# One maximum over two score banks: PSUM as one tile of eight banks in a fused attention and feed-forward kernel

## The chip, the core and the metric

One core of a Trainium2 chip runs the whole program. The metric is the device time of one execution in microseconds (us). Lower is better.

The engines are named as in the profile. PE is TensorE, with PEld for its weight loads. DVE is VectorE, ACT is ScalarE, POOL is GpSimd, and SP issues the DMAs. PSUM is the memory that PE writes its results to: eight banks, of which one holds 512 float32 numbers in each of 128 partitions.

## The reference

Attention over 8 batches of 12 heads, 448 positions, 64 numbers a head, followed by a feed-forward layer over all 3584 positions:

```python
q_n, k_n = rmsnorm(q, g_q), rmsnorm(k, g_k)          # over the last axis
scores = (q_n @ k_n.T) / sqrt(64)
scores = scores - max(scores, axis=-1)
attn = exp(scores); attn = attn / (sum(attn, axis=-1) + 1e-9)
x = (attn @ v)                                       # heads joined: 3584 x 768
h = relu(x @ w_in)                                   # 768 x 2048, float64 weights
out = (s * h * h + b) @ w_out                        # 2048 x 768
```

## The kernel before

The kernel works on 48 pairs of heads, six pairs to a batch. A pair has eight steps (`W = 8`), four for each of its two heads. One Python loop over the step number `s_`, from -16 on, writes out the order of the work of every engine by hand, and each engine then runs its own queue strictly in that order. What is called "step s" below is one turn of this loop.

For each pair the scores are computed twice. The first time is only for the maxima. `score(i)` multiplies a block of 112 queries of one head with all 448 keys of that head (PE L453) into a PSUM bank (`sh`), and `maximum(i)` takes the negated maximum of each query out of it (DVE L464) into one column of `nmx`. A pair has eight such blocks, `i = 8 * pair + 0 ... 7`, and this holds for the first twelve pairs (`TURNED = 12`). `shift` then sends four columns at a time by DMA into a row of `qb`. The second time, `score_t(s)` computes one transposed block of 128 keys by 448 queries, with the maxima already subtracted (PE L496 and L499, bank `st`), `exponent(s)` takes the exponential (ACT L511), and `weigh(s - 2)` multiplies with the values, summing four steps in one bank `av` (PE L557, two instructions a step). `take` copies `av` out (ACT L568, L572, L573).

Queries and keys come in as rows. `norm_rows` scales them (ACT L255, DVE L260, POOL L263, L264 and L269), `turn` transposes them on PE into two banks (`tk`, L282, two groups of four), and `split_turned` makes the high and low parts out of the two banks (ACT L290, L291 and L292; one step later DVE L294 and L295). For four steps at a time this runs at a fixed distance: the transposes in a step that is 2 more than a multiple of 4, L290 to L292 in the next step, L294 and L295 in the step after, which is a multiple of 4.

Beside this, DVE turns pieces of the float64 weights `w_in` into float32 parts (`convert`, DVE L149, L152, L154 and L157 for each piece, 24 pieces), and from step 56 on the feed-forward matmuls of the batch before (PE L198, names `ph`) fill PE's queue between the others. So during the first six pairs, steps 0 to 47 and some more, PE has no such filler.

The order inside one step is: `score_t`, filler, `exponent`, what was begun earlier (L260, L294, L295 among it), the jobs of the step (turns among them), `score`, filler, `maximum`, the late jobs (`convert` among them), `weigh`, filler.

A block's step is `i - AHEAD` with `AHEAD = 10`. The first 20 blocks have steps of their own in `SHIFTED`: 0 to 19 stand at -9, -8, -7, -6, -4, -3, -2, -1, 1, 1, 2, 2, 4, 4, 5, 5, 8, 8, 9, 10.

A bank is taken by `psum()`, which pops the one that stands first in the list `free`, and is appended to the list again where the code gives it back. Because the list is one queue over all uses, a PE instruction into a bank waits for the last reader of whatever used that bank before: an `exponent` (ACT), a `take` (ACT), an L295 (DVE) or a `maximum` (DVE).

Of the kernel before, what the change touches and what calls it, by code (L numbers as in the profile page):

```python
# [9 lines left out]
F32 = mybir.dt.float32  # L10
# [3 lines left out]
ALU = mybir.AluOpType  # L14
AX = mybir.AxisListType
# [10 lines left out]
AHEAD = 10  # L26
# [11 lines left out]
SHIFTED = {0: -9, 1: -8, 2: -7, 3: -6, 4: -4, 5: -3, 6: -2, 7: -1, 8: 1, 9: 1, 10: 2, 11: 2, 12: 4, 13: 4, 14: 5, 15: 5, 16: 8, 17: 8, 18: 9, 19: 10}  # L38
# [13 lines left out]
PLAIN = 11  # L52

THIRD = (11, 14, 17)

PACE_OUT = tuple(48 * b + 16 + 8 * i for b in range(2, 8) for i in range(4))

# [4 lines left out]
def attention_then_relu2_ffn(  # L62
# [30 lines left out]
    V, S, G, T = nc.vector, nc.scalar, nc.gpsimd, nc.tensor  # L93

    NPAIR, P, _, SEQ = kq.shape
# [10 lines left out]
    QC = SEQ // NQ  # L106
# [16 lines left out]
    wpool = ctx.enter_context(tc.tile_pool(name="wpool", bufs=1))  # L123
    dpool = ctx.enter_context(tc.tile_pool(name="dpool", bufs=1, space=DRAM))
    ps = ctx.enter_context(tc.tile_pool(name="ps", bufs=1, space=PSUM))
    free = [f"bank{i}" for i in range(8)]

    ident = cpool.tile([P, P], F32, name="ident")
    make_identity(nc, ident)
# [11 lines left out]
    def psum(name):  # L141

        bank = free.pop(0)
        return ps.tile([P, 512], F32, tag=bank, name=name), bank

    def to_single(w, a, m):

# [29 lines left out]
    def parts_of_w_in():  # L177

        for i in range(NS):
            whi[i] = wpool.tile([P, NCC, FS], F32R, tag=f"wh{i}", name=f"wih{i}")  # L180
            wlo[i] = wpool.tile([P, NCC, FS], F32R, tag=f"wl{i}", name=f"wil{i}")
            for c0 in range(0, FS, WI):
                for cc in range(NCC):
                    f0 = 2 * (i * FS + c0)
                    src = w_in32[cc * P : (cc + 1) * P, f0 : f0 + 2 * WI]
                    yield whi[i][:, cc, c0 : c0 + WI], wlo[i][:, cc, c0 : c0 + WI], src
# [4 lines left out]
    def ffn_in(xs, b, fcs):  # L191

        phs = [psum(f"ph{b}_{fc}") for fc in fcs]
        for cc in range(NCC):
            for (ph, bank), fc in zip(phs, fcs):
                i, f0 = divmod(fc * P, FS)
                for m, (w, part) in enumerate(((whi[i], 0), (wlo[i], 0), (whi[i], 1))):
                    T.matmul(  # L198
                        ph[:, :SEQ],
                        w[:, cc, f0 : f0 + P],  # L200
                        xs[b, cc][:, part, :],
                        start=cc == 0 and m == 0,
                        stop=cc == NCC - 1 and m == 2,
                    )
                    if cc == NCC - 1 and m == 2:
                        later.append((ph, bank, b, fc))
                    yield
# [22 lines left out]
    with tc.tile_pool(name="apool", bufs=1) as ap:  # L230
        khs = {}
        raws, kqs, invs, vrs, nmxs, shs, tks = ({} for _ in range(7))
# [38 lines left out]
        def turn(p, j):  # L271
            raw = raws.pop((p, j))
            if p >= APART:
                tk, bank = tks[p, j] = psum(f"tk{p}_{j}")
                for c in range(NQ):
                    x = raw[:, c].rearrange("p t d -> p (t d)")
                    T.transpose(tk[:, c * QC : (c + 1) * QC], x, ident[:QC, :QC])
                return
            for t in range(2):
                tk, bank = psum(f"tk{p}_{j}_{t}")  # L280
                for c in range(NQ):
                    T.transpose(  # L282
                        tk[:D, c * QC : (c + 1) * QC], raw[:, t, c], ident[:QC, :QC]
                    )
                tks[p, j, t] = tk[:D, :SEQ], bank
# [151 lines left out]
        def score(i):  # L437

            p, c = divmod(i, W)
            j, c = divmod(c, NQ)  # L440
            sh, bank = psum(f"sh{i}")
            a = slice(j * SEQ, (j + 1) * SEQ)
            shs[i] = sh, bank
            if p >= TURNED:
                q, k = qz, khs.get(p)
                if i % W != 3:
                    q = qa[p % 2][:, a][:, :WHOLE].rearrange("k (p c) -> k c p", c=3)[:, c]
                    k = ka[p % 2][:, a]
                else:
                    khs.pop(p)  # L450
                T.matmul(sh[:, :SEQ], q, k, start=True, stop=True)  # L451
                return
            T.matmul(  # L453
                sh[:QC, :SEQ], qa[p % 2][:, a].rearrange("k (p c) -> k c p", c=NQ)[:, c],
                ka[p % 2][:, a], start=True, stop=True,
            )

        def maximum(i):
            p, c = divmod(i, W)
            if c == 0:  # L460
                nmxs[p] = bounds.tile([P, W], F32R, tag="nmx", bufs=2, name=f"nmx{p}")
            sh, bank = shs.pop(i)
            n = QC if p < TURNED else P
            V.tensor_reduce(  # L464
                out=nmxs[p][:n, c : c + 1], in_=sh[:n, :SEQ], op=ALU.max, axis=AX.X, negate=True
            )
            free.append(bank)
# [158 lines left out]
        def pieces():  # L626
            for i, (hi, lo, src) in enumerate(parts_of_w_in()):
                if i in THIRD:
                    w = ap.tile([P, WI, 2], I32, tag="low", name=f"w64i{i}")
# [72 lines left out]
        def at(s_, f, *a):  # L702
            jobs[s_].append((f, a))

        for i, s_ in enumerate(PACE):
            if i != THIRD[-1]:
                at(s_ + 3, load_piece)
# [64 lines left out]
        scores = {}  # L772
        for i in range(NSLOT):
            if i // W >= TURNED and i % W == W - 1:
                continue
            scores.setdefault(SHIFTED.get(i, i - AHEAD), []).append(i)

        def within(i):
            return 0 <= i < NSLOT
# [2 lines left out]
        with tc.manual_schedule(engines=ORDERED):  # L782
            begun = []
            for s_ in range(FIRST, NSLOT + START + NCC):
# [20 lines left out]
                for i in scored:  # L805
                    score(i)
# [4 lines left out]
                for i in scored:  # L811
                    maximum(i)
# [14 lines left out]
    with tc.tile_pool(name="opool", bufs=1) as op:  # L827
# [153 lines left out]
        with tc.manual_schedule(engines=ORDERED):  # L981
# [29 lines left out]
            for n in range(7 * NG):  # L1011
                g, k = divmod(n, 7)
# [78 lines left out]
```

## Time and profile before

| what | value |
|---|---|
| time, median of 3 runs | 1376.97 us (1376.26 to 1377.02) |
| span of the profiled execution, first to last instruction | 1375.6 us |
| median less span (launch and end around the span) | 1.4 us |
| PE busy in the span | 1363.6 us (99%) |
| DVE busy in the span | 1057.3 us (77%) |
| ACT busy in the span | 937.2 us (68%) |
| granted TensorE clock over the span | 1.000 |

The page gives no other time of the profiled execution than its span, so the median is set beside the span here. PE's matmuls are pipelined, so that a busy share of 99% doesn't say that PE never waits: how far the starts of its instructions lie apart says more. The same holds for DVE, where the record of an instruction lasts some 0.08 us longer than it keeps the next one away.

### The profile page before, as it was taken

The page shows a single profiled execution, that of the slowest core. Times are in us where ns is not written, and L with a number is a line of the kernel's source. Part 1 is how long each engine was busy: PE and PEld are TensorE (multiplying, and loading weights), DVE is VectorE, ACT ScalarE, POOL GpSimd, SP SyncE. Part 2 cuts the span into 40 slices and gives each one's busy share as a digit, 9 for nine tenths or more (in the row PEclk, how much of TensorE's full clock was granted, in tenths as well). Part 3 has the DMA queues.
Part 4 walks back from the last instruction along what each step waited for, and adds up shares of the span by engine and source line. Part 5 has one row for each costly group of instructions (what it writes and reads, how often), then busy time and mean ns, then how long its engine had stood idle before and what let it go on. Part 6 is the DMA issues. An engine that isn't in the chain of part 4 may idle for free.

```text
span 1375.6 us, 21578 instructions
## 1 busy us (share of the span) xinstructions
PE 1363.6 (99%) x6970; PEld 1255.6 (91%) x6970; DVE 1057.3 (77%) x1572; ACT 937.2 (68%) x1727; POOL 603.1 (44%) x486
## 2 busy tenths in 40 slices
PE   8999999999999999999999999999999999999998
PEld 7767789999999999999999999999999999999998
DVE  7999997897888798688788878526766676666763
ACT  6886778888888888888888887636544434344431
POOL 6875787766667666676667665100000000000000
PEclk9999999999999999999999999999999999999999
DMA  4555676787788788778778867356543332343330
GB/s 133 150 145 169 181 232 197 230 249 214 223 235 239 222 243 232 221 222 250 229 220 240 236 204 211 104 197 222 186 119 118 88 91 90 95 121 112 85 90 35
DMA packets 262800, 243.39 MB, mean 177 GB/s; under 512 B 85280, under 2 KB 244000, under 8 KB 262688
## 3 DMA queue, kind: packets, MB, share of 16 engines
q1 hardware_dynamic: 262688, 242.03, 60.0%
q8 instruction: 55, 0.90, 0.3%
q14 instruction: 57, 0.47, 0.1%
HBM read 177.21 MB, written 53.38 MB: 168 GB/s over the span
## 4 chain that ended last, share of the span: by engine, by line
PE 92%; DVE 4%; ACT 2%; DMA 1%; issue 1%; SPq 0%; POOL 0%; DVEq 0%; POOLq 0%; ACTq 0%
PE ph L198 32%; PE p L936 30%; PE av L557 15%; PE st L496 5%; PE st L499 5%; PE sh L451 4%; PE sh L453 1%; DVE nmx L464 1%; PE tk L282 1%; DVE wai L154 1%; DVE ssq L260 0%; DVE wai L152 0%; DVE wai L157 0%; DMA zb<-z_d 0%; ACT e L511 0%
## 5 line engine op out<-in xcount | busy, mean ns | idle before, releaser
L198 PE MATMUL ph<-x,wih 128*128 128x448 f32 x1536 | 488.3, 365 | 0.0
L198 PEld LDWEIGHTS ph<-x,wih 128*128 128x128 f32 x1536 | 289.0, 188 | 28.7 <-issue 6.1
L198 PE MATMUL ph<-x,wil 128*128 128x448 f32 x768 | 293.3, 382 | 0.0
L515 ACT ACTIVATE st<-st 128x448 f32<-128x448 f32 (+1 forms) x296 | 155.9, 527 | 104.1 <-PE st L499 102.7
L464 DVE TENSOR_REDUCE nmx<-sh 128x1 fp32r<-128x448 f32 (+1 forms) x348 | 212.8, 616 | 12.0 <-PE sh L451 6.3
L538 DVE TENSOR_TENSOR low<-st,ah 128x448 fp32r<-128x448 f32 x222 | 136.7, 616 | 47.2 <-ACT ah L523 42.5
L557 PE MATMUL av<-ah,vs 128*128 128x448 f32 x592 | 168.7, 366 | 0.0
L496 PE MATMUL st<-qa,ka 128*128 128x448 f32 (+1 forms) x384 | 159.1, 414 | 2.3 <-DVE nmx L464 2.2
L198 PEld LDWEIGHTS ph<-x,wil 128*128 128x128 f32 x768 | 144.3, 188 | 17.0 <-issue 6.2
L523 ACT CAST ah<-st 128x448 fp32r<-128x448 f32 (+1 forms) x296 | 156.9, 530 | 2.0
L499 PE MATMUL st<-qb,kb 128*128 128x448 f32 (+1 forms) x384 | 140.3, 365 | 0.0
L557 PEld LDWEIGHTS av<-ah,vs 128*128 128x128 f32 x592 | 111.2, 188 | 8.6
L921 ACT CAST hi<-a 128x1024 fp32r<-128x1024 f32 x54 | 56.8, 1053 | 91.0 <-PE p L936 74.0
L420 POOL TENSOR_TENSOR ka<-kq,ka 64x448 fp32r<-64x448 f32 x72 | 86.2, 1198 | 56.3 <-ACT ka L415 53.0
L603 POOL TENSOR_TENSOR u<-uz,zb 128x448 f32<-128x448 f32 x48 | 59.9, 1247 | 95.9 <-DMA zb<-z_d 75.9
L421 POOL TENSOR_TENSOR qb<-kq,qa 64x448 fp32r<-64x448 f32 x72 | 95.3, 1323 | 5.4
L369 POOL TENSOR_TENSOR ri<-ri,mhalf 128x14 f32<-128x14 f32 x36 | 93.6, 2601 | 3.0
L922 DVE TENSOR_TENSOR lo<-s,hi 128x1024 fp32r<-128x1024 f32 x41 | 50.1, 1222 | 52.1 <-ACT hi L921 52.1
L218 ACT ACTIVATE r<-ph 128x448 f32<-128x448 f32 x128 | 69.7, 545 | 27.6 <-PE ph L198 15.8
L354 POOL TENSOR_TENSOR vs<-vr,vs 128x512 fp32r<-128x512 f32 x37 | 49.4, 1336 | 86.0 <-DMA w64o<-in_dram 31.4
L496 PEld LDWEIGHTS st<-qa,ka 128*128 128x128 f32 (+1 forms) x384 | 68.2, 178 | 20.2 <-DVE nmx L464 6.1
L385 POOL TENSOR_TENSOR kq<-kq,rb 128x448 f32<-128x448 f32 x72 | 86.5, 1202 | 0.0
(253 smaller groups left out, 3256.4 us busy)
## 6 DMA issues: line engine op xcount, KB each, us to landing
kq<-in_dram SPq DMA_DIRECT2D x72, 448.0 KB, 5.1
rb<-i_d SPq DMA_DIRECT2D x72, 448.0 KB, 4.8
r_d<-r SPq DMA_DIRECT2D x128, 224.0 KB, 3.7
a<-r_d SPq DMA_DIRECT2D x48, 512.0 KB, 4.9
raw<-in_dram SPq DMA_DIRECT2D x36, 448.0 KB, 5.0
w64i<-in_dram SPq DMA_DIRECT2D x24, 512.0 KB, 4.5
w64o<-in_dram SPq DMA_DIRECT2D x48, 256.0 KB, 4.1
kb<-ka SPq DMA_DIRECT2D x96, 112.0 KB, 2.8
```

The source lines that it names most:

```text
L198: T.matmul(ph[:, :SEQ], w[:, cc, f0 : f0 + P], xs[b, cc][:, part, :], start=cc == 0 and m == 0, stop=cc == NCC - 1 and m == 2,)
L369: G.tensor_tensor(ri, ri, mhalf[:, :n], ALU.pow)
L385: G.tensor_tensor(t[:, 0], t[:, 0], rb[:, 0], ALU.mult)
L421: G.tensor_tensor(qb[n][:D, a], t[:D, 1], qa[n][:D, a].bitcast(F32), ALU.subtract)
L464: V.tensor_reduce(out=nmxs[p][:n, c : c + 1], in_=sh[:n, :SEQ], op=ALU.max, axis=AX.X, negate=True)
L496: T.matmul(st[:rows, :SEQ], ka[n][:, keys], qa[n][:, q], start=True, stop=False)
L499: T.matmul(st[:rows, :SEQ], kb[n][:, keys], qb[n][:, q], start=False, stop=True,)
L515: S.activation(st[:rows, :SEQ], st[:rows, :SEQ], AF.Exp)
L523: S.copy(ah[:rows], sts[i][0][:rows, :SEQ])
L538: V.tensor_tensor(al, st[:rows, :SEQ], ah[:rows].bitcast(F32), ALU.subtract)
L557: T.matmul(av[:, :SEQ], x, a, start=kc == 0 and m == 0, stop=kc == 3 and m == len(todo) - 1,)
L936: T.matmul(po, a[:, f], w[:, f], start=f == 0 and m == 0, stop=f == NH - 1 and m == 2,)
```

## The change

PSUM becomes one tile `space` of eight banks, in place of eight tiles. The list `free` holds banks 0 to 5 at first. Banks 6 and 7 are set aside for the first 48 blocks of queries (`WIDE`, six pairs): an even block goes to bank 6 and the odd block after it to bank 7, both in the step of the even one. `maximum` does nothing for the even block, and for the odd block one operation reads both banks (112 partitions, 2 times 448 numbers) and writes two columns of `nmx`. After block 47 the banks 6 and 7 join the list, and from block 48 on everything goes as before. So the pairs of blocks stand at the steps -9, -7, -4, -2, 1, 2, 4, 5, 8, 9, 10, 12, 14 and so on to 36.

```diff
+WIDE = 8 * 6
...
-    free = [f"bank{i}" for i in range(8)]
+    space = ps.tile([P, 8, 512], F32, name="space")
+    free = list(range(6))
...
         bank = free.pop(0)
-        return ps.tile([P, 512], F32, tag=bank, name=name), bank
+        return space[:, bank], bank
...
-            sh, bank = psum(f"sh{i}")
+            sh, bank = (space[:, 6 + i % 2], None) if i < WIDE else psum(f"sh{i}")
...
             sh, bank = shs.pop(i)
+            if i < WIDE:
+                if i % 2:
+                    V.tensor_reduce(
+                        out=nmxs[p][:QC, c - 1 : c + 1], in_=space[:QC, 6:, :SEQ],
+                        op=ALU.max, axis=AX.X, negate=True,
+                    )
+                if i == WIDE - 1:
+                    free.extend((6, 7))
+                return
...
-            scores.setdefault(SHIFTED.get(i, i - AHEAD), []).append(i)
+            k = i // 2 * 2 if i < WIDE else i
+            scores.setdefault(SHIFTED.get(k, k - AHEAD), []).append(i)
```

## Rows read from the trace of the kernel before

**Rows 1.** Busy time by stage: length, PE, PEld, DVE, ACT, POOL, granted clock, DMA.

```profile
10.00:34.00 24.00, 22.66 (x117) 17.50 (x117) 20.86 (x36) 17.82 (x35) 15.26 (x17) 1.00 0.54 150
34.00:68.00 34.00, 33.87 (x149) 24.66 (x149) 32.57 (x63) 29.55 (x59) 27.37 (x24) 1.00 0.54 148
68.00:139.00 71.00, 67.25 (x286) 49.28 (x284) 68.37 (x111) 56.17 (x109) 46.84 (x38) 1.00 0.56 157
139.00:870.00 731.00, 730.51 (x3557) 662.78 (x3558) 616.08 (x989) 611.51 (x1263) 500.93 (x388) 1.00 0.77 224
```

**Rows 2.** The chain that ended last, in order of time: start, length, piece.

```profile
35.03 0.75 PE av L557 x2
...
138.58 0.64 DVE nmx L464
...
444.58 4.00 DMA zb<-z_d
```

**Rows 3.** PE's groups from 68 to 139 us that waited for the maxima.

```profile
L496 PE MATMUL st<-qa,ka 128*128 128x448 f32 x34 | 20.7, 609 | 1.6 <-DVE nmx L464 1.6
L453 PE MATMUL sh<-ka,qa 128*112 128x448 f32 x35 | 14.9, 427 | 1.8 <-DVE nmx L464 1.1 <-DVE ka L310 0.6
```

**Rows 4.** One of DVE's groups from 34 to 139 us: busy, mean ns.

```profile
L154 DVE SCALAR_TENSOR_TENSOR wai<-w64i,wai 128x512 int32<-128x512 int32 x13 | 12.9, 993 | 0.0
```

**Rows 5.** DVE in order of time: start, duration, instruction, count, idle before.

```profile
13.14 0.62 DVE L294 TENSOR_TENSOR ka<-tk,ka 64x448 fp32r<-64x448 f32 x1
...
17.32 0.62 DVE L294 TENSOR_TENSOR ka<-tk,ka 64x448 fp32r<-64x448 f32 x1
...
19.16 2.20 DVE L464 TENSOR_REDUCE nmx<-sh 112x1 fp32r<-112x448 f32 x4
...
30.18 0.68 DVE L295 SCALAR_TENSOR_TENSOR qb<-tk,singles,qa 64x448 fp32r<-64x448 f32 x1 [0.56 <-ACT qa L292]
30.78 1.14 DVE L464 TENSOR_REDUCE nmx<-sh 112x1 fp32r<-112x448 f32 x2
...
33.49 0.61 DVE L464 TENSOR_REDUCE nmx<-sh 112x1 fp32r<-112x448 f32 x1
...
37.58 0.68 DVE L295 SCALAR_TENSOR_TENSOR qb<-tk,singles,qa 64x448 fp32r<-64x448 f32 x1
38.18 0.61 DVE L464 TENSOR_REDUCE nmx<-sh 112x1 fp32r<-112x448 f32 x1
...
45.19 0.61 DVE L464 TENSOR_REDUCE nmx<-sh 112x1 fp32r<-112x448 f32 x1
```

**Rows 6.** DVE later: a reduction over 896 numbers and its successor.

```profile
153.51 1.07 DVE L365 TENSOR_REDUCE ssq<-raw 128x14 f32<-128x896 f32 x1
154.51 0.61 DVE L464 TENSOR_REDUCE nmx<-sh 112x1 fp32r<-112x448 f32 x1
```

**Rows 7.** PE in order of time, without its weight loads.

```profile
10.06 0.77 PE L453 MATMUL sh<-ka,qa 128*112 128x448 f32 x2 [0.50 <-ACT qa L292]
...
18.08 0.74 PE L453 MATMUL sh<-ka,qa 128*112 128x448 f32 x2 [0.28 <-DVE ka L294]
...
19.07 0.57 PE L453 MATMUL sh<-ka,qa 128*112 128x448 f32 x2
...
30.48 0.37 PE L453 MATMUL sh<-ka,qa 128*112 128x448 f32 x1
...
34.16 0.47 PE L496 MATMUL st<-qa,ka 128*128 128x448 f32 x1
...
42.36 0.36 PE L453 MATMUL sh<-ka,qa 128*112 128x448 f32 x1
...
45.76 0.54 PE L453 MATMUL sh<-ka,qa 128*112 128x448 f32 x1
```

**Rows 8.** ACT in order of time, around step 11.

```profile
34.94 0.54 ACT L511 ACTIVATE e<-st 128x448 f32<-128x448 f32 x1 [1.34 <-PE st L499]
...
36.43 0.63 ACT L292 ACTIVATE qa<-tk,singles 64x448 fp32r<-64x448 f32 x1
```

## The prediction, as it was put down before the changed kernel was timed

> **What bounds the kernel now.** I read busy time by stage first, then the chain of work, then the engines' instructions in order of time. By stage, PE is full from 139 us on [rows 1]: whatever delays the start of that stage is added to the end one to one. The chain says the same: its last piece that is not PE before 444 us is a maximum on DVE at 138.58 [rows 2], so DVE hands over to PE there. Before it there are three regimes [rows 1]. From 34 to 68 us PE has 33.87 of 34 us, with DVE close behind (32.57). From 68 to 139 DVE is the fullest (68.37 of 71) and PE has gaps, 2.7 us of them behind maxima [rows 3]. From 10 to 34 neither is full: there PE and DVE wait for each other in turn. The change acts on steps -9 to 37, the first two regimes and the first 10 us of the third. The range within which a timing of this kernel can't be told from no change I take as 0.2%, 2.75 us.
>
> **What the wide maximum saves.** In a run of four maxima the starts lie (2.20 - 0.61) / 3 = 0.53 us apart [rows 5]; two cost DVE 1.06. A reduction over 896 numbers holds DVE for 154.51 - 153.51 = 1.00 and its record lasts 1.07 [rows 6]. It reads SBUF and not two PSUM banks, but it is the nearest row. So a pair saves 0.06, and 24 pairs 1.4 us. Bounds: nothing, if two banks cost as two operations; and at most 24 x (0.61 - 0.53) = 1.9 more, if the tail of one record, which now overlaps its successor, counted as well.
>
> [...] By the rows 448 numbers more take 1.00 - 0.53 = 0.47, so the fixed part of a maximum is 0.53 - 0.47 = 0.06. [...] I take the 1.4 of the rows, since only the distance of starts is engine time.
>
> The single tile itself I cost at nothing: the banks, the readers and who waits for whom are the same. So is the moving of odd blocks one step ahead: a score issues no DMA, and `shift` keeps its step.
>
> **What the change adds: a wait on PE.** Until now the next scores take another bank out of eight. Now every pair goes into banks 6 and 7, so its scores can't start before the wide maximum of the pair ahead has ended: 1.07 after that one's start, and 0.06 more, as between a maximum and the PE instruction that it releases (33.49 + 0.61 to 34.16) [rows 5, 7]. PE works in order, so `weigh`, the next `score_t` and with it ACT's exponent queue behind the scores. Pairs two steps apart have room. But the early pairs stand in neighbouring steps (1 and 2, 4 and 5, 8, 9 and 10), and I follow these by hand.
>
> *Steps -9 to 0.* The first two scores end at 10.06 + 0.77 = 10.83 [rows 7]; the wide maximum starts at 10.87 and ends at 11.94. The next two scores, 0.74 long, run from 12.0 to 12.75, the second wide maximum from 12.79 to 13.86, and L294 behind it starts at 13.9 in place of 13.14 [rows 5]. Scores follow L294's end by 0.14 (17.32 + 0.62 to 18.08): 14.7 to 15.4. Then maximum 15.45 to 16.5, scores 16.6 to 17.35, maximum from 17.4 to 18.45, and the next L294 at 18.45 in place of 17.32: 1.1 late.
>
> *Steps 1 and 2.* L294, L295 and a sum take DVE from 17.32 to 19.16 before the maxima [rows 5], 1.84. So the wide maximum of step 1 starts at 20.3 and ends at 21.37, and the scores of step 2 start at 21.43 in place of 19.07 [rows 7]: **2.4 us late**. Even undelayed DVE would give 19.16 + 1.13 = 20.3, 1.2 late. Steps 4 and 5 add about 0.1, since the first maximum ends just when the second scores are due: 2.5.
>
> *Steps 8 to 10.* L295 of step 8 waits for ACT and so for PE [rows 5]: 30.18 + 2.5 = 32.7. The wide maximum starts 0.6 later, 33.3, and ends at 34.35. The scores of step 9 would start at 30.48 + 2.5 = 33.0 [rows 7]; they start at 34.4, **1.4 more**. Between the maxima of steps 8 and 9 DVE has 33.49 - 30.78 - 1.06 = 1.65 of other work [rows 5], so the wide maximum of step 9 runs from 33.3 + 1.0 + 1.65 = 35.95 to 37.0, and the scores of step 10 start at 37.1. Two scores (0.4) and the two L557 (0.75 [rows 2]) later the `st` of step 11 starts at 38.25 in place of 34.16 [rows 7]: 4.1 late, and **3.9** from there on, because step 11 has lost its score of 0.2.
>
> *What DVE has lost by then.* The exponent of step 11, and L292 two instructions behind it, come 4.1 later: L292 ends at 36.43 + 0.63 + 4.1 = 41.15 [rows 8]. L295 must wait for it, which it did not (37.58), and the maximum of step 12 starts 0.6 later, at 41.75 in place of 38.18 [rows 5]: **DVE 3.6 late**.
>
> **From step 12 to 139 us.** The pairs now lie two steps apart. One of the three worst of the pairs of steps 12 to 36 has its maximum at 45.19, with scores at 42.36 and the next pair's at 45.76 [rows 5, 7]: 45.19 + 1.13 = 46.3 is 0.55 too late. But DVE has come 3.9 - 3.6 = 0.3 nearer to PE and gains 0.06 a pair, so I count nothing for these waits. DVE then has 13 pairs to save 0.06 on, 0.8: it reaches 139 us 3.6 - 0.8 = 2.8 late if it never starves. PE arrives 3.9 late in the third regime, but has more than 2.7 us of waits behind maxima there to give [rows 3], so DVE decides. For some starving behind the later PE I add 0.2 out of the 1.1 between the two. **Sum: 3.0 us later.** Span 1375.6 + 3.0 = 1378.6, and with the 1.4 that the median of the runs lies above the span, 1380.0.
>
> The own range of this case is 1378.0 to 1382.0. The wide maximum at its bounds moves the sum by 1.5 at most to either side. And L154 takes 0.99 in the mean [rows 4], where L295, a form of nearly its size, takes 0.68 [rows 5]: thirteen of these alone carry 4 us of disturbance, which may fall otherwise when the engines shift against each other.
>
> **Rivals.**
>
> *The late start is taken in* (0.28). DVE was idle for 0.56 before one L295, and has such holes elsewhere [rows 5, 1]: 24.0 - 20.86 = 3.1 between 10 and 34. If these swallow the first waits, only those of steps 9 and 10 remain: 1.4 + 0.4 - 0.8 = 1.0, so 1378.0. For it: holes of that size. Against it: most of them come from ACT and PE, which are late too.
>
> *DVE's saving wins* (0.09). If the maxima end before the next scores are due, DVE, which sets the end of the third regime, keeps its 1.4, and of PE's waits behind maxima, 2.7 [rows 3], anything up to all could go, because `st` and `tk` take no bank from a maximum any more until step 38. That is 1.4 to 4.1, in the middle 2.8: 1374.2. It turns on one place: the wide maximum of step 1 must end before 19.07, and the narrow one only starts at 19.16 [rows 5, 7], which speaks against it.
>
> *The whole record of a maximum is engine time* (0.03). Then two narrow ones cost 1.22 and a wide one 1.07, and DVE saves 0.15 on each of the 13 pairs from step 12 on, 2.0 in place of 0.8: 3.0 - 1.2 = 1.8 later, 1378.8. Against it: the starts 0.53 apart. [...]
>
> *The wait recurs* (0.16). If DVE doesn't come nearer to PE, the three worst pairs cost 0.4 to 0.55 each, about 1.5, and PE's delay of 3.9 stays whole: 3.9 + 1.5 = 5.4, less what DVE saves, 0.8: 4.6, so 1381.6. For it: PE is full from 34 to 68.
>
> *PE's longer holes lower the granted clock* (0.04). It is 1.00 in all stages [rows 1], and PE loses up to 3.9 us of work before 38 us. [...]
>
> **Chances.** My forecast has 0.40. Of it I give 0.24 to over 2.75 us, 0.16 to under. Slower: 0.24 + 0.16 + 0.04 + 0.02 (the tail of the first rival) = 0.46. Same: 0.16 + 0.26 + 0.03 (of the second rival) + 0.03 = 0.48. Faster: 0.06, the rest of the second rival. The range 1376.0 to 1382.8 holds the forecast, the first and third rival and most of the recurring wait, and leaves out the gain, the lowered clock and the tails.
>
> **What would show it.** The maxima of the pairs as 24 reductions of 2 x 448, about 1.07 long. PE idle ahead of a pair's scores, released by a wide maximum, at about 20.4 to 21.4, 33.1 to 34.4 and around 37, and the `st` of step 11 at about 38.2. The last piece of DVE in the chain at about 141.6, and PE full behind it. It is wrong if these scores start without a wait; if the waits stand there and the last DVE piece still comes at 139; if the wide maximum's record is far from 1.07; or if the granted clock leaves 1.00.

## The result, and the profile after

Changed kernel: **1386.72 us**, median of five runs (1385.12 to 1387.61), against 1377.02 for the kernel before (1376.26 to 1379.80). The ratio is 1.0066 with a 95% interval of 1.0055 to 1.0077: slower by 0.66%, 9.7 us. The forecast was 1380.0, and the top of its range 1382.8. The sign of the forecast was right, its size was not.

The profiled execution took 1387.35 us, its span 1385.2 (before 1375.6). Busy time by stage of the changed kernel (length, PE, PEld, DVE, ACT, POOL, granted clock, DMA), beside [rows 1]:

```profile
10.00:34.00 24.00, 20.58 (x100) 15.09 (x100) 17.47 (x22) 15.02 (x29) 14.91 (x16) 1.00 0.47 130
34.00:68.00 34.00, 32.15 (x139) 23.18 (x140) 30.53 (x47) 27.88 (x56) 22.54 (x18) 1.00 0.51 138
68.00:139.00 71.00, 65.20 (x275) 46.92 (x274) 67.94 (x106) 55.71 (x108) 51.62 (x41) 1.00 0.49 140
139.00:870.00 731.00, 729.59 (x3547) 660.52 (x3546) 613.00 (x986) 610.09 (x1260) 503.95 (x390) 1.00 0.77 225
```

PE has lost work in each of the first three stages: 22.66 - 20.58 = 2.1, then 1.7, then 2.05. The clock is 1.00 throughout. So the loss isn't one event at the start; a third of it falls behind 68 us, where only the last five of the 24 wide maxima lie. The chain of work, in order of time (start, length, piece), beside [rows 2]:

```profile
33.74 0.22 PE space L511
33.96 0.05 issue
34.01 1.08 DVE nmx L468
35.09 0.04 issue
35.14 0.77 PE space L456 x2
...
147.85 0.64 DVE nmx L476
```

The wide maximum (L468 now, the narrow one L476) stands in the chain where the prediction put it, ahead of the scores of step 9. But the last piece of DVE comes at 147.85: 9.3 later than the 138.58 of before, where the forecast had 3.0. PE in order of time (scores L456, `weigh` L569, `st` L508 and L511; idle time before, and what ended it, in brackets), beside [rows 7]:

```profile
21.50 0.78 PE L456 MATMUL space<-ka,qa 128*112 128x448 f32 x2 [1.06 <-DVE nmx L468]
...
29.80 1.02 PE L569 MATMUL space<-e,vf 128*128 128x448 f32 x2
...
35.14 0.77 PE L456 MATMUL space<-ka,qa 128*112 128x448 f32 x2 [1.19 <-DVE nmx L468]
...
37.80 0.77 PE L456 MATMUL space<-ka,qa 128*112 128x448 f32 x2
...
39.35 0.36 PE L511 MATMUL space<-qb,kb 128*128 128x448 f32 x1
...
51.13 0.77 PE L456 MATMUL space<-ka,qa 128*112 128x448 f32 x2 [0.41 <-DVE nmx L468]
...
74.99 0.78 PE L456 MATMUL space<-ka,qa 128*112 128x448 f32 x2 [0.84 <-DVE nmx L468]
```

DVE in order of time, beside [rows 5]:

```profile
13.90 0.62 DVE L297 TENSOR_TENSOR ka<-space,ka 64x448 fp32r<-64x448 f32 x1
...
20.37 1.07 DVE L468 TENSOR_REDUCE nmx<-space 112x2 fp32r<-112x896 f32 x1
...
34.01 1.07 DVE L468 TENSOR_REDUCE nmx<-space 112x2 fp32r<-112x896 f32 x1
35.01 0.41 DVE L152 TENSOR_SCALAR wai<-w64i 128x512 int32<-128x512 int32 x1
...
36.66 1.08 DVE L468 TENSOR_REDUCE nmx<-space 112x2 fp32r<-112x896 f32 x1
...
42.57 1.07 DVE L468 TENSOR_REDUCE nmx<-space 112x2 fp32r<-112x896 f32 x1
...
70.58 2.09 DVE L599 TENSOR_SCALAR zt<-zt 128x7 f32<-128x7 f32 x1
...
127.29 3.36 DVE L157 SCALAR_TENSOR_TENSOR wai<-w64i,wai 128x512 int32<-128x512 int32 x1
...
138.50 3.92 DVE L155 SCALAR_TENSOR_TENSOR wai<-w64i,wai 128x512 int32<-128x512 int32 x1
```

The first waits are as forecast: L297 at 13.90 (13.9), the wide maximum of step 1 at 20.37 (20.3), the scores of step 2 at 21.50 (21.43). A wide maximum takes 1.07, and the next instruction starts 35.01 - 34.01 = 1.00 after it. The scores of step 10 too start 0.06 behind a wide maximum (36.66 + 1.08 to 37.80). The last three lines of DVE are a sum over 7 numbers a partition that takes 2.09 us, and two conversions that take 3.36 and 3.92 (some 0.68 elsewhere). In the kernel before the same three operations are L587, in order of time, and L154 and L152, here from the chain of work, where a piece can start a little later than the record (3.27 in the chain of the change for the one of 3.36):

```profile
65.47 0.17 DVE L587 TENSOR_SCALAR zt<-zt 128x7 f32<-128x7 f32 x1 [0.23 <-issue]
```

```profile
118.77 3.28 DVE wai L154
...
129.90 2.67 DVE wai L152
```

So the conversion of 3.36 is not new; the long sum is, and the last conversion has grown by 1.25. Beside the first two POOL had this to do:

```profile
70.28 1.14 POOL L615 TENSOR_TENSOR u<-uz,zb 128x448 f32<-128x448 f32 x1
71.38 1.27 POOL L173 TENSOR_TENSOR wil<-wai,wih 128x512 fp32r<-128x512 f32 x1
...
126.24 1.51 POOL L272 TENSOR_TENSOR rows<-rows,ri 112x512 f32<-112x512 f32 x1
127.71 1.15 POOL L615 TENSOR_TENSOR u<-uz,zb 128x448 f32<-128x448 f32 x1
128.81 1.29 POOL L173 TENSOR_TENSOR wil<-wai,wih 128x512 fp32r<-128x512 f32 x1
```

The sum ends at 72.67, and POOL's L173 at 72.65. The long conversion ends at 130.65, and the last of POOL's three operations at 130.10, about one undisturbed conversion (0.68) earlier. In both places DVE's operation lasted until POOL's had ended; what held it there these rows don't show.

### The profile page after: what moved, and what is told of

Same layout as the page of the kernel before. It is cut to its first block, busy times and chain, and to the rows that moved or that the text cites. A ratio compares the mean times of both kernels' runs of the same rounds, so it can differ in the third digit from the quotient of the medians.

```text
span 1385.2 us, 21426 instructions
## 1 busy us (share of the span) xinstructions
PE 1366.3 (99%) x6970; PEld 1255.8 (91%) x6970; DVE 1056.7 (76%) x1548; ACT 937.7 (68%) x1727; POOL 606.9 (44%) x486
## 4 chain that ended last, share of the span: by engine, by line
PE 93%; DVE 4%; POOL 1%; ACT 1%; DMA 1%; issue 1%; DVEq 0%; POOLq 0%; ACTq 0%
PE space L201 33%; PE space L949 29%; PE space L569 15%; PE space L508 5%; PE space L511 5%; PE space L454 4%; PE space L456 1%; DVE nmx L468 1%; PE space L285 1%; DVE wai L157 1%; POOL ri L267 0%; DVE nmx L476 0%; DVE x L628 0%; DVE ssq L263 0%; DVE wai L160 0%
## 5 line engine op out<-in xcount | busy, mean ns | idle before, releaser
L201 PE MATMUL space<-x,wih 128*128 128x448 f32 x1536 | 488.4, 365 | 0.0
L201 PEld LDWEIGHTS space<-x,wih 128*128 128x128 f32 x1536 | 288.9, 188 | 28.8 <-issue 6.1
L201 PE MATMUL space<-x,wil 128*128 128x448 f32 x768 | 293.4, 382 | 0.0
L527 ACT ACTIVATE space<-space 128x448 f32<-128x448 f32 (+1 forms) x296 | 156.0, 527 | 103.3 <-PE space L511 101.7
L476 DVE TENSOR_REDUCE nmx<-space 128x1 fp32r<-128x448 f32 (+1 forms) x300 | 184.5, 616 | 12.3 <-PE space L454 6.7
L569 PE MATMUL space<-ah,vs 128*128 128x448 f32 x592 | 168.7, 366 | 0.0
L508 PE MATMUL space<-qa,ka 128*128 128x448 f32 (+1 forms) x384 | 159.3, 415 | 2.2 <-DVE nmx L476 2.2
L201 PEld LDWEIGHTS space<-x,wil 128*128 128x128 f32 x768 | 144.3, 188 | 17.1 <-issue 6.2
L535 ACT CAST ah<-space 128x448 fp32r<-128x448 f32 (+1 forms) x296 | 156.9, 530 | 2.0
L511 PE MATMUL space<-qb,kb 128*128 128x448 f32 (+1 forms) x384 | 140.3, 365 | 0.0
L569 PEld LDWEIGHTS space<-ah,vs 128*128 128x128 f32 x592 | 111.2, 188 | 8.6
L508 PEld LDWEIGHTS space<-qa,ka 128*128 128x128 f32 (+1 forms) x384 | 68.2, 178 | 19.5 <-issue 7.3
```

The lines of the kernel that those rows point to most:

```text
L201: T.matmul(ph[:, :SEQ], w[:, cc, f0 : f0 + P], xs[b, cc][:, part, :], start=cc == 0 and m == 0, stop=cc == NCC - 1 and m == 2,)
L476: V.tensor_reduce(out=nmxs[p][:n, c : c + 1], in_=sh[:n, :SEQ], op=ALU.max, axis=AX.X, negate=True)
L508: T.matmul(st[:rows, :SEQ], ka[n][:, keys], qa[n][:, q], start=True, stop=False)
L511: T.matmul(st[:rows, :SEQ], kb[n][:, keys], qb[n][:, q], start=False, stop=True,)
L527: S.activation(st[:rows, :SEQ], st[:rows, :SEQ], AF.Exp)
L535: S.copy(ah[:rows], sts[i][0][:rows, :SEQ])
```

## The experiments

A measure used throughout is how late the second `st` instruction of a step starts against the kernel before (34.47 us at step 11, 147.31 at step 70), by the traces. Part of a lateness is there from the start: kernels that do the same work up to step 7 as the change are 1.4 to 2.2 late at step 1 and 3.2 to 3.9 at step 7, so differences below 0.7 between two traces say little, and growth within one trace says more. Another measure is how much DVE is *drawn out* between these two steps: over its records, the time of each less the shortest of its line, where that is 0.05 us or more. In the kernel before it is 11.6 us, of which 9.4 lie beside POOL's subtraction L170 (L173 now). That an operation lies beside one of POOL's says little by itself, since 133 of the 164 that aren't drawn out do so too. But 13 of the 16 drawn-out ones of the kernel before, and 11 of the 14 of the change, end just one undisturbed duration (to 0.13 us) after an operation of POOL ended, and the others are drawn out by less than 0.1 us each.

The texts on record name four theories. A: the scores wait for the one pair of banks. B: the list of six runs dry for `st`, `tk` and `av`. C: the wide operation, or the odd block's earlier step, costs by itself. D: the single tile adds waits. From the second group on, L and N say whose the loss from step 12 on is, DVE's or PE's. The medians stand beside those of the kernel before on the same chip (1376.96 to 1377.93). The edits are shown in part, against the change unless the text says otherwise; "..." marks lines left out.

**One tile alone.** The kernel before with its banks in one tile: list of eight, and without the change's branch for the wide maximum and its line for `k`.

```diff
-    free = list(range(6))
+    free = list(range(8))
...
-            sh, bank = (space[:, 6 + i % 2], None) if i < WIDE else psum(f"sh{i}")
+            sh, bank = psum(f"sh{i}")
...
```

> PSUM as one tile, all else as before (a list of eight banks, one maximum for each block, the old steps). Theories of the 9.7 us: A, scores wait for the one set-aside pair of banks; B, the list of six banks runs dry for st, tk and av; C, the wide operation, or the odd block's earlier step, costs by itself; D, the single tile adds waits. A, B and C expect 1377 (within 0.2%); D expects most of the 9.7, about 1385.

1377.49, ratio 1.0003 [0.9994, 1.0012]. D falls.

**The wide maximum over any two banks of the list.**

```diff
-    free = list(range(6))
+    free = list(range(8))
...
+                if i % 2 == 0:
+                    two[:] = sorted((free.pop(0), free.pop(0)))
...
-                        out=nmxs[p][:QC, c - 1 : c + 1], in_=space[:QC, 6:, :SEQ],
+                        out=nmxs[p][:QC, c - 1 : c + 1],
+                        in_=space[:QC, lo : hi + 1 : hi - lo, :SEQ],
...
+                    free.extend((lo, hi))
```

> The wide maximum and the earlier step of odd blocks as in the change, but each pair takes any two banks out of the list of eight, so that nothing is set aside. A and B expect the loss gone and the saving of DVE left over: 1374 to 1378. C expects about 1386.

1407.5, ratio 1.022 [1.0206, 1.0234], where 1374 to 1378 or 1386 were expected. It tells nothing about A, because it brought a wait of its own. PE of this kernel in order of time (`st` L519, `weigh` L580, wide maximum L479):

```profile
23.65 0.47 PE L519 MATMUL space<-qa,ka 128*128 128x448 f32 x1 [2.75 <-DVE nmx L479]
...
36.19 1.12 PE L580 MATMUL space<-e,vf 128*128 128x448 f32 x1 [2.40 <-DVE nmx L479]
```

`st` and `av` wait for the wide maximum, though neither takes a bank that it reads: by the list in the code, they use bank 1 while it reads 0 and 5, and bank 3 while it reads 0 and 6. The profile ends these waits with a semaphore of the maximum, so they stand in the program; whether PSUM itself would hold the writers up is not shown. From 68 to 139 us the granted clock was 0.93 here.

**Set aside, but two narrow maxima.** As the change, with the old reduction of one block each.

```diff
-                if i % 2:
-                    V.tensor_reduce(
-                        out=nmxs[p][:QC, c - 1 : c + 1], in_=space[:QC, 6:, :SEQ],
+                V.tensor_reduce(
+                    out=nmxs[p][:QC, c : c + 1], in_=sh[:QC, :SEQ],
...
```

> Banks 6 and 7 set aside and the list of six as in the change, odd blocks a step ahead, but one narrow maximum for each block. The first score of a pair now waits only for the first maximum of the pair ahead, which ends 0.47 us sooner than the wide one, and the second for the second. A expects most of the loss to stay, some 4 to 9 us over before (1381 to 1386). B expects 1386. C, if it is the wide operation, expects 1377.

**Only the odd block's step.** Against the first experiment, with the change's line for `k`:

```diff
-            k = i
+            k = i // 2 * 2 if i < WIDE else i
```

> A list of eight banks and narrow maxima as before, but odd blocks of the first six pairs a step ahead, as in the change. A, B and D expect 1377 (within 0.3%). C, if it is the step, expects several us more, 1380 to 1386.

The first gave 1381.49 (1.0031 [1.0019, 1.0042]), the second 1378.59 (1.0011 [1.0002, 1.002]). In the traces they are 3.6 and 0.6 late at step 11, and 4.1 and 0.8 at step 70. So of the 4.9 that the full change has lost by step 11, added in this order, 0.6 come from the step, 3.0 from setting the pair aside and 1.3 from the wide operation, for whose whole length the even block's bank is held too. The 3.0 hold A and B together: the traces show A's waits, and about 0.3 of B in step 6 (below). After step 11 both lose next to nothing; the full change loses 4.3 more. For that B isn't enough, since the list of six is the same in the narrow kernel.

**Only the first three pairs of heads, or only the last three of the six.**

```diff
-WIDE = 8 * 6
+WIDE = 8 * 3
```

> The change for the first three pairs alone (24 blocks, steps -9 to 12, where pairs of blocks stand in neighbouring steps); from block 24 on a list of eight and narrow maxima at the old steps. A, with the loss in the close early steps, expects PE 4.9 us late at step 11 as in the change and little added behind it: 1380 to 1383. If the later steps make most of the loss: 1377 to 1379. B, for which the list of six runs dry all along, expects about half of the loss, 1381 to 1382.

For the late half, two neighbouring banks are taken from the list at block 24 and given back behind block 47:

```diff
-            sh, bank = (space[:, 6 + i % 2], None) if i < WIDE else psum(f"sh{i}")
+            if EARLY <= i < WIDE:
...
+                sh, bank = space[:, two[i % 2]], None
+            else:
+                sh, bank = psum(f"sh{i}")
...
-            k = i // 2 * 2 if i < WIDE else i
+            k = i // 2 * 2 if EARLY <= i < WIDE else i
```

> The opposite: as before up to block 23, then for blocks 24 to 47 (steps 14 to 36) two neighbouring banks set aside, a list of six and wide maxima. If the early steps carry the loss: 1377 to 1379, perhaps 1376 for the saving of DVE. If the wait recurs in the later steps, 1380 to 1382. The two losses should add to about 9.7.

1383.96 (1.0045 [1.003, 1.006]) and 1382.11 (1.0033 [1.0021, 1.0045]). The first lies 1.0 above A's range. It is 5.3 late at step 11 and 5.1 at steps 23, 37 and 50, so next to nothing is taken in; at step 70 it is 6.0 late, though no wide maximum stands behind step 12. The second is 0.2 late at step 11 and 5.1 at step 70. So there are two losses, and either half makes one of 5 us or more by itself. But they were expected to add up to the whole, and they don't: 7.0 and 5.2 above the kernel before make 12.2, where the change loses 9.7.

**Blocks 16 to 23 further apart.** All pairs of blocks at least two steps apart from step 7 on:

```diff
-16: 8, 17: 8, 18: 9, 19: 10}
+16: 7, 17: 7, 18: 9, 19: 9, 20: 11, 21: 11, 22: 13, 23: 13}
```

> The change, with blocks 16 to 23 in pairs at the steps 7, 9, 11 and 13 in place of 8, 9, 10 and 12, so that no two of these pairs stand in neighbouring steps. A expects the waits of steps 9 and 10 gone, PE about 3 us late at step 11 in place of 4.9, and 1384 to 1385 in the end. B and C expect no gain, 1386 to 1387.

1386.37 (1.0061 [1.0044, 1.0078]). At step 11 it is 1.7 better than the change, as A has it (3.2 late); by step 23 it is 5.9 late, at step 70 8.2. In time it stands 9.4 above the kernel before, so A's 1384 to 1385 is missed: the early gain is lost again.

**Two pairs set aside alternately**, banks 4, 5 and 6, 7, with a list of four.

```diff
-    free = list(range(6))
+    free = list(range(4))
...
-            sh, bank = (space[:, 6 + i % 2], None) if i < WIDE else psum(f"sh{i}")
+            sh, bank = (space[:, 4 + i % 4], None) if i < WIDE else psum(f"sh{i}")
...
-                        out=nmxs[p][:QC, c - 1 : c + 1], in_=space[:QC, 6:, :SEQ],
+                        out=nmxs[p][:QC, c - 1 : c + 1], in_=space[:QC, 3 + i % 4 : 5 + i % 4, :SEQ],
...
-                    free.extend((6, 7))
+                    free.extend((4, 5, 6, 7))
```

> Two pairs of banks set aside in turn (4 and 5, 6 and 7), so that a score no longer waits for the maximum just ahead of it; the list for st, tk and av has only four banks. A expects the waits of scores behind maxima gone and the time at 1377 to 1381 if four banks suffice. B expects the shorter list to cost more than the change does: 1388 to 1400, with PE waiting for exponents and for L298.

1389.33 (1.0086 [1.0071, 1.0101]), as B has it. Step 11 gains 1.6 here too, and step 23 is 8.6 late: four banks for the rest are too few. From 10 to 90 us the first `st` instructions wait 4.3 us for exponents, in 10 places; in the change none of them does.

**Neighbours out of the list of eight.** Against the second experiment: two banks that lie side by side, with nothing between them.

```diff
-                    two[:] = sorted((free.pop(0), free.pop(0)))
+                    both = [b for b in free if b + 1 in free]
+                    lo = min(both, key=lambda b: max(free.index(b), free.index(b + 1)))
+                    two[:] = lo, lo + 1
...
-                        in_=space[:QC, lo : hi + 1 : hi - lo, :SEQ],
+                        in_=space[:QC, lo : hi + 1, :SEQ],
```

> As the change, but nothing is set aside: every pair takes two neighbouring banks out of the list of eight, and one operation takes their maxima. Theory A (the loss is made by the one pair of banks that every pair must use): the early pairs find other banks, the st of step 11 comes 1 to 2 us later than before in place of 4.9, and the end about 2 to 4 later, 1379 to 1381. Theory C (the wide operation and the odd block's earlier step cost by themselves): the later steps still lose about 4 us, so 1382 to 1385. A rival to both: taking two neighbours makes the list run dry or out of order, and st and av wait: 1386 and more.

1382.9 (1.0037 [1.0024, 1.005]), in C's range and above A's. Step 11 is 2.4 late in place of 4.9, so by this comparison half of the early loss, 2.5, belongs to the fixed pair (with its list of six); the later stretch still loses 2.6.

**A delay of PE alone**, in the kernel before.

```diff
-HEAT = {FIRST: 16, -11: 4, -5: 4}
+HEAT = {FIRST: 16, -11: 4, -5: 4, 11: 15}
```

> The kernel before, with 15 warm-up calls (about 4.0 us of PE alone) ahead of step 11: PE is late, DVE loses nothing of its own work and banks are as before. Rigid theory: from step 11 on the engines run in a chain that has no slack, the delay reaches the end whole, 3.6 to 4.3 later, 1380.6 to 1381.3. Absorption (the prediction's reading of the third regime, where DVE sets the end and PE has 2.7 us of waits to give): 1 to 2.7 later, 1378 to 1379.7.

1380.94, ratio 1.0024 [1.0014, 1.0034], 3.3 above the kernel before and in the rigid theory's range. Its trace, in order of time on PE and DVE:

```profile
34.07 3.62 PE L329 MATMUL warmth<-ident 128*128 128x128 f32 x30
37.45 0.45 PE L496 MATMUL st<-qa,ka 128*128 128x448 f32 x1
38.34 0.62 DVE L464 TENSOR_REDUCE nmx<-sh 112x1 fp32r<-112x448 f32 x1 [2.07 <-PE sh L453]
```

The `st` of step 11 comes 37.45 - 34.16 = 3.3 late, DVE waits 2.07 for the scores, and step 70 is still 3.0 late. So 0.3 of 3.3 is taken in from step 11 on, though PE has its 2.7 us behind maxima in the third regime [rows 3]. These waits don't shrink: from 39 to 148 us they are 3.1 us here and 3.3 in the kernel before. DVE is drawn out by 11.6 as before: this delay doesn't disturb it.

**DVE made light**, in both kernels.

```diff
-        V.scalar_tensor_tensor(a, high, -0x40000000, a, ALU.bitwise_and, ALU.bitwise_or)
...
-        V.scalar_tensor_tensor(a, low, 29, a, ALU.logical_shift_right, ALU.bitwise_or)
...
-        V.scalar_tensor_tensor(af, m.bitcast(F32), LEAST * LEAST, af, ALU.is_ge, ALU.mult)
```

> The kernel before with the three two-input operations of each conversion left out (the weights are then wrong numbers); DVE has about 33 us less to do between 34 and 139. It is the base for the next run. All theories: PE alone sets the pace, 1368 to 1374.

> The changed kernel with the same three operations left out. Theory L (the 4 us that are lost from step 12 on are DVE's: its other operations are drawn out beside POOL, and its maxima come late): only the early loss stays, so it lies 4 to 5.5 above the light kernel before. Theory N (they are PE's own waits for the pair of banks and for the list of six, whatever DVE's load): it lies 8 to 10 above it, as the full one does. If even the early loss goes (below 3), the early waits too came from DVE's load.

1371.01 and 1376.37: 5.4 apart in place of 9.7 (spans 6.8 apart in place of 9.6). By stage, the light kernel before and then the light changed one:

```profile
34.00:68.00 34.00, 34.00 (x151) 24.79 (x149) 25.08 (x49) 30.33 (x60) 24.52 (x23) 1.00 0.53 146
68.00:139.00 71.00, 71.00 (x313) 54.93 (x312) 49.52 (x90) 61.19 (x120) 45.66 (x43) 1.00 0.62 177
```

```profile
34.00:68.00 34.00, 32.96 (x145) 24.10 (x145) 23.60 (x36) 28.65 (x58) 22.25 (x21) 1.00 0.55 152
68.00:139.00 71.00, 71.00 (x314) 54.42 (x313) 49.45 (x88) 61.35 (x121) 48.77 (x45) 1.00 0.58 168
```

PE is full in both, but for the wait of step 9 in the second. The changed one lies 5.1 behind at step 11 and 5.0 at step 70, and never off by more than 0.2 in between. So the early loss doesn't depend on these conversions, and the later loss does: L, not N. With DVE light, the pair of banks cost PE nothing after step 12. Whether it is DVE's amount of work or its meetings with POOL that matters, these two don't say; the last experiment does.

**Without the small sums.** The sum of 1e-9 in `invert` left out of the changed kernel.

```diff
-            V.tensor_scalar(zt, zt, 1e-9, None, ALU.add)
```

> The changed kernel without the seven sums of 1e-9 on the 128 x 7 divisors, one of which takes 2.09 us on DVE beside two operations of POOL (0.16 alone). Collision theory (the later loss comes from DVE operations that are drawn out beside POOL): this one's 2 us come back, 1384 to 1385. Rival (DVE just meets the next collision or waits for PE or ACT in its place): no more than 0.6 us comes back, 1385.8 to 1387.

1384.43 (1.0044 [1.0029, 1.0059]). The number is that of the collision theory, but not for its reason. DVE of this kernel at the same place:

```profile
70.50 0.18 DVE L599 RECIPROCAL zt<-zt 128x7 f32<-128x7 f32 x1
70.60 2.25 DVE L152 TENSOR_SCALAR wai<-w64i 128x512 int32<-128x512 int32 x1
```

The next operation stands in the sum's place and ends at 72.85, behind the same two of POOL's, of which the later one ends at 72.57. Step 28 is only 0.1 better. What came back came at steps 52 to 67, where other collisions fell otherwise (14.1 us drawn out, 15.5 with the sums).

**POOL without its subtraction**, in both kernels.

```diff
-        G.tensor_tensor(dst_lo, a.bitcast(F32), dst_hi.bitcast(F32), ALU.subtract)
+        S.copy(dst_lo, a.bitcast(F32))
```

> The kernel before with POOL's subtraction of each weight piece's high part left out: ACT writes a copy in its place, 0.6 us more for ACT a piece (the low parts are then wrong). Of the 11.6 us by which DVE's operations are drawn out between steps 11 and 70, 9.4 lie beside this subtraction. It is the base for the next run: 1369 to 1376.

> The changed kernel with the same subtraction left out. Collision theory: the early loss of about 5 stays and of the later 4 at most 1.5, so 5 to 6.5 above the run before it. Rival (the later loss is waiting: DVE's maxima late for the pair of banks, whatever POOL does): 8 to 10 above it, as in the full kernels.

1376.3 (just above what was expected) and 1381.68: again 5.4 apart, as the collision theory has it. Between the two, step 11 is 4.9 late and step 70 5.8, so of the later loss 0.9 is left. DVE is drawn out by 5.6 and 6.3.

An account of DVE's time says the same for the full kernels. From its maximum of step 12 (38.18 and 42.57) to its last piece in the chain (138.58 and 147.85) it does the same work in both, but for the merged maxima. The stretch is 100.4 us in the kernel before and 105.3 in the change, 4.9 more: 3.9 more drawn out, 1.3 more idle, and 0.3 less of all else. With the pair set aside and narrow maxima it is 101.5, with the same 1.3 more idle and 0.3 less drawn out. So what the full change has on top of that kernel is time that DVE is drawn out.

Put together, the stretch from step 11 to step 70 (us) and DVE's drawn-out time in it:

| kernel | length | drawn out |
|---|---|---|
| before | 112.8 | 11.6 |
| one tile; step only; set aside, narrow | 112.4; 113.0; 113.4 | 11.9; 11.8; 11.8 |
| PE delayed | 112.6 | 11.6 |
| first three pairs of heads | 113.5 | 13.0 |
| neighbours from the list | 115.5 | 14.1 |
| the change | 117.2 | 15.5 |
| last three pairs of heads | 117.7 | 15.7 |
| blocks 16 to 23 spaced; two pairs of banks | 117.8; 121.0 | 14.7; 16.6 |
| no subtraction: before, change | 110.7, 111.6 | 5.6, 6.3 |
| light: before, change | 106.2, 106.1 | 1.9, 1.9 |

## Why the prediction was right or wrong

- **The first waits: right.** The wide maximum's record (1.07), the distance behind it (1.00), the scores of steps 2, 9 and 10 behind a wide maximum. The single tile at nothing: right. The granted clock: right. The odd blocks' earlier step, also put at nothing, costs 0.6 by step 11 on its own.
- **PE's lateness: 4.9 at step 11 for 4.1, and 4.7 behind it for 3.9, mis-sized by 0.8.** DVE's follows it: its maximum of step 12 comes at 42.57 for 41.75, 4.4 late for 3.6. Two small terms were missed. Steps 4 and 5 cost 0.4, not 0.1. And in step 6 `av` (29.80) stood about 0.3 behind the exponent of its own step, because a list of six hands out banks in another order.
- **The step that failed is the one from step 12 to 139 us: DVE would lose nothing more and save 0.8, and PE's 2.7 us of waits would take in its delay, so that DVE would reach 139 us 2.8 late.** To this it added 0.2. DVE's last piece came 9.3 late. Of the 6.3 that the sum of 3.0 was short, 0.8 is the term above, and the rest arose here: DVE took 105.3 us where the sum has 99.9.
- **The larger error is in DVE's other work, which the sum takes to last as before.** A wide maximum does hold DVE 0.06 less than two narrow ones. But the other operations were drawn out by 3.9 more, and idle time grew by 1.3. With DVE light the later loss is gone, and with POOL's subtraction away it falls from 4.3 to 0.9. The prediction had this risk, as 4 us in [rows 4] that "may fall otherwise". It read them off one line, where all lines together had 11.6 us, and kept them out of the sum and of most of the range. Here they were larger than the forecast itself.
- **The smaller error is that PE's waits are room: worth at most 0.9, from PE's 3.9 down to the sum's 3.0.** The delayed kernel shows that 3.0 of 3.3 go through to step 70, and the early half alone that its 5.3 are still 5.1 at step 50. PE and DVE were not two clocks of which the later one counts. DVE waits for PE's scores, PE then for DVE's maxima, and a delay of PE moves both.
- **The wait recurs** (1381.6) is the nearest of the rivals in its mechanism, and right that PE's delay stays whole. Its price, three pairs of 0.4 to 0.55, isn't there in the light kernels. In the full one four such waits stand, 2.1 us in all (0.41 at 51.13, 0.84 at 74.99, soon after the long sum), behind a DVE that is late.
- *The late start is taken in* and *DVE's saving wins* fell: no hole swallowed a wait, and the wide maximum of step 1 ended at 21.44, not before 19.07. *The lowered clock* fell too: the clock stayed at 1.00 in all four stages. *The whole record is engine time* fell with the distance of 1.00.

Early 4.9 and later 4.3 make 9.2 at step 70, and 9.3 in the last DVE piece of the chain. Two things stay open. Why DVE and POOL fall against each other worse with wide maxima wasn't settled: the five other kernels with wide maxima out of neighbouring banks, DVE and POOL whole, were all drawn out more (13.0 to 16.6), the four with narrow ones not (11.6 to 11.9). But the one with strided reads had 10.2, at a clock that had fallen (0.95 from 34 to 68 us, 0.93 from 68 to 139). And the early half has no wide maxima behind step 12, so that its 13.0 can't come from them; perhaps it comes from the late start of 5.3, though the delay of 3.3 brought nothing. And the table doesn't run one to one: in the kernel before, taking 6.0 away gave back only 2.1.

## What to carry to other kernels

Where two engines feed each other step by step, count an early delay in full unless a run shows that it is taken in; idle time of one behind the other was no room here (of a delay of 3.3 us, 3.0 went through). Before merging two small operations into a wider one, ask what its buffers are held for: here 1.4 us of forecast saving stood against 4.9 us of early loss, of which 2.5 to 3.0 came from setting aside one pair of banks. And where operations are drawn out beside another engine, a shift of order can move the sum of it by several us (here from 11.6 to 15.5): that belongs into the range.

## What was not expected of the hardware

With a read at a stride over two banks, writers of the banks between them waited for it (2.40 and 2.75 us, 1407.5 in all), by semaphores of the program. A collision of DVE with POOL belonged to its place in time and not to the instruction: with the sum over 7 numbers (2.09) gone, the next one took 2.25 and ended at 72.85 in place of 72.67. And one operation of DVE, begun at 127.29, ended at 130.65 only, behind the third of POOL's operations in a row (130.10).
